# Moving the loads of the next batch's k and v behind the last store of a second layer

## The chip, the cores and the metric

The kernel runs on one core of one Trainium2 chip. The metric is the device time of one execution in microseconds (us). A single-core run gets the state "fast" unless it is over 1.5% above the fastest run of the same kernel.

## The reference

Linear attention without softmax, an RMS norm, then a gated feed-forward layer, all in fp32:

```python
# q, k, v: (8 batches, 8 heads, 576 tokens, 64)
kv  = einsum('bhsd,bhse->bhde', k, v)
out = einsum('bhsd,bhde->bhse', q, kv)
out = out / sqrt(mean(out*out, -1) + 1e-6) * g_norm
x   = out.transpose(0, 2, 1, 3).reshape(4608, 512)
gate = 1 / (1 + exp(-(x @ w_gate)));  val = x @ w_val          # 512 -> 1536
result = (gate * val) @ w_out                                  # 1536 -> 512
```

## The kernel before

The feed-forward layer goes over nine chunks of 512 tokens, c = 0 to 8. Each chunk has a first layer (`first_layer_fast`, pairs of blocks of 7 products each) and a second layer (`second_layer_fast`). The products of both are of a Strassen kind: 7 in place of 8. The attention of batch c+1 is fed into chunk c in small steps: a queue `fill`, from which `slot()` takes one step after each pair of products.

What the argument needs: k and v of batch c+2 are asked for at the end of chunk c, and used in chunk c+1.

```python
def load_late(b):                      # 12 transfers, all on SP's queue
    if b >= B: return
    for n in range(NHP):               # 8 of 128 x 512 fp32 (256 KB)
        for name, src in (("k", k), ("v", v)):
            mains[n, name] = t = hp.tile([P, G], FP32, tag="gv", name="kv")
            nc.sync.dma_start(out=..., in_=src[b, 2*n:2*n+2, 0:S4]...)          # L112
    rest = hp.tile([P, G], FP32, tag="gv", name="kv")
    for i, src in enumerate((k, v)):   # 4 of 64 KB
        for r in range(2):
            nc.sync.dma_start(out=rest[...], in_=src[b, ..., S4:S]...)          # L117
...
def feed(b):                           # steps of the attention of batch b, for fill
    ...
    steps = turns_of(n0) + turns_of(n0 + 1)        # 4 transposes on DVE
    if b > 2:
        steps += [(PE, idle)] * (7 - len(steps))
    steps += [(PE, kv_mm), (DVE, kv_out)]          # the k.v products: L347, L353
...
def sg_tile():
    return sb.tile([P, G], FP32, tag="sg", name="sg", bufs=4)
...
def first_layer_fast(c):               # in each block
    d["pa"] = pa = mm_ps()[:, h1]
    product(pa, bg[:, 0:NK], a[1, 1], True)                     # L693
    d["sg"] = sg_tile()
    nc.scalar.copy(out=d["sg"][:, h2], in_=pa)                  # L701: writes an sg buffer
    ...
def second_layer_fast(c):
    for g in range(2):
        ...                                                     # o2, o1 = sg_tile(), sg_tile()
        store(c, 2 + g, o2)
        if g == 1:
            load_late(c + 2)
        for pc, x in zip(pcs, parts):
            product(pc, lambda f: s4[c, f][:, t1], b[2, 2][:, :, x], False)
            tt(out=o1[:, y], in0=pc, in1=o1[:, y], op=ALU.add)  # L811
            ...
        if not last:
            store(c, g, o1)                                     # L488, L493
```

The pool `sg` has four buffers, A to D. The built program hands them out in a fixed round: the second layer's four tiles take C, B, A, D (o2 and o1 of g = 0, then o2 and o1 of g = 1), each read by a store. The next first layer's first pair of blocks takes C and B, its second pair A and D. So the L701 of the eighth step of that first layer writes D, the buffer that the last store reads.

Of the kernel before, what the change touches and what calls it, by code (L numbers as in the profile page):

```python
# [20 lines left out]
def kernel(  # L21
# [81 lines left out]
    def load_late(b):  # L103


        if b >= B:
            return
        mains = {}
        for n in range(NHP):
            for name, src in (("k", k), ("v", v)):  # L110
                mains[n, name] = t = hp.tile([P, G], FP32, tag="gv", name="kv")
                nc.sync.dma_start(out=t.rearrange("p (h c) -> p h c", h=2),  # L112
                                  in_=src[b, 2 * n:2 * n + 2, 0:S4].rearrange("h (p j) d -> p h (j d)", j=NK4))
        rest = hp.tile([P, G], FP32, tag="gv", name="kv")
        for i, src in enumerate((k, v)):
            for r in range(2):
                nc.sync.dma_start(out=rest[PH * r:PH * r + PH, GH * i:GH * i + GH].rearrange("p (h d) -> p h d", d=HD),  # L117
                                  in_=src[b, NHP * r:NHP * r + NHP, S4:S].rearrange("h p d -> p h d"))
        kv_late[b] = mains, rest
# [209 lines left out]
    def slot():  # L329
        if fill:  # L330
            fill.popleft()()
# [144 lines left out]
    def sg_tile():  # L476
        return sb.tile([P, G], FP32, tag="sg", name="sg", bufs=4)

    def store(c, t, ot, cols=slice(0, DM), queues=(nc.sync,)):

        r0 = i = 0
        while r0 < P:
            b, s = divmod(G * c + P * t + r0, S)
            rows = out[S * b:S * b + S, cols]
            if b < 2:
                j, p = divmod(s, NP)
                n = min(P - r0, NP - p)
                queues[i % len(queues)].dma_start(out=rows.rearrange("(p j) d -> j p d", j=NJ)[j, p:p + n],  # L488
                                                  in_=ot[r0:r0 + n, cols])
            else:  # L490
                r, c0 = divmod(s, QC)
                n = min(P - r0, QC - c0)
                queues[i % len(queues)].dma_start(  # L493
                    out=rows.rearrange("(r p j) d -> r j p d", p=QB, j=NJ)[r, c0 // QB:(c0 + n) // QB],
                    in_=ot[r0:r0 + n, cols])
            r0 += n
            i += 1
# [12 lines left out]
    def mm_ps():  # L510
        if next(turns) % 4 < 2:
            return psum.tile([P, 512], FP32, tag="mm", name="mm", bufs=2)
        return mm0_ps()
# [253 lines left out]
    def second_layer_fast(c):  # L767
        b = {(j, n): w2[:, NF2 * (j - 1):NF2 * j, DH * (n - 1):DH * n] for j in (1, 2) for n in (1, 2)}
        d1, d2 = slice(0, DH), slice(DH, DM)
        for g in range(2):  # L770
            t1, t2 = slice(P * g, P * g + P), slice(GH + P * g, GH + P * g + P)
            pa, pb = (mm_ps()[:, 0:DH] for _ in range(2))

            last = (c, g) == (NG - 1, 1)
            parts = [slice(0, DH // 2), slice(DH // 2, DH)] if last else [slice(0, DH)]

            def product(ps, hs, ws, new):
                for f in range(NF2):
                    nc.tensor.matmul(ps, hs(f), ws[:, f, :], start=(new and f == 0), stop=(f == NF2 - 1),  # L779
                                     skip_group_check=True)  # L780
                    if f % 3 == 2:
                        slot()

            product(pa, lambda f: gv[c, f][:, t1], b[1, 1], True)
            o2 = sg_tile()
            nc.scalar.copy(out=o2[:, d1], in_=pa)
            product(pb, lambda f: s12[c, f][:, t2], t2w[2], True)
            o1 = sg_tile()
            tt(out=o1[:, d2], in0=pb, in1=o2[:, d1], op=ALU.add)
            product(pa, lambda f: gv[c, f + NF2][:, t1], b[2, 1], False)  # L790
            nc.scalar.copy(out=o1[:, d1], in_=pa)
            if last:
                store(c, g, o1, d1)
            product(pb, lambda f: gv[c, f][:, t2], t2w[3], False)
            tt(out=o2[:, d2], in0=pb, in1=o2[:, d1], op=ALU.add)
            pcs = []
            for x in parts:
                pcs.append(mm_ps()[:, 0:x.stop - x.start])
                pc = pcs[-1]
                product(pc, lambda f: s12[c, f][:, t1], t2w[1][:, :, x], True)  # L800
                o2x = o2[:, DH + x.start:DH + x.stop]
                tt(out=o2x, in0=pc, in1=o2x, op=ALU.add)
            product(pb, lambda f: gv[c, f + NF2][:, t2], t2w[4], False)
            tt(out=o2[:, d1], in0=pb, in1=o2[:, d1], op=ALU.add)
            store(c, 2 + g, o2)
            if g == 1:
                load_late(c + 2)
            for pc, x in zip(pcs, parts):
                product(pc, lambda f: s4[c, f][:, t1], b[2, 2][:, :, x], False)
                y = slice(DH + x.start, DH + x.stop)  # L810
                tt(out=o1[:, y], in0=pc, in1=o1[:, y], op=ALU.add)  # L811
                if last:
                    store(c, g, o1, y, (nc.sync, nc.scalar))
            if not last:
                store(c, g, o1)

    def sums_of(c):
        if c < NG:
            fill.append(lambda: fill.extendleft(reversed(x_sums(c))))
# [31 lines left out]
    for c in range(1, NG):  # L851
        if c + 1 < B:
            steps = feed(c + 1)
            if c == 1:

                i = 5
                while w2_sums:
                    steps.insert(i, (DVE, w2_sums.popleft()))
                    i += 3
            spread(steps, (1, 2, 3, 4, 5) if c == 1 else (2, 3, 4, 5))  # L860
        first_layer_fast(c)
        sums_of(c + 1)
        second_layer_fast(c)
        flush()
# [30 lines left out]
```

## Time and profile before

| | |
|---|---|
| median of 4 runs | 1098.61 us (1098.3 to 1099.22) |
| span of the profiled run | 1100.3 us, granted clock 0.995 |
| TensorE (PE) busy | 98% |
| PE's waits for L701 | 6.0 us, 4 times |

In the profile PE is TensorE, ACT ScalarE, DVE VectorE, SP the engine whose queue issues the transfers. L693 is a line of the kernel. A wait row reads "engine, line that waited <- what released it: us in total, times, longest". A timeline row reads "start, duration, engine, line, operation, out<-in, count, [idle before <- releaser]"; "SPq" is SP's queue, and its duration is the issue alone. In the rows of windows the seventh value after the window's ends is the granted clock. The prediction shows the page, PE's waits, the chain and SP's queue; here is what it read without showing: ACT and PE at the end of chunk 2 in the timeline of the kernel before.

```profile
411.37 0.37 ACT L701 COPY sg<-mm 128x256 f32<-128x256 f32 x1 [1.71 <-PE mm L693]
...
414.75 0.37 ACT L701 COPY sg<-mm 128x256 f32<-128x256 f32 x1 [3.00 <-DMA out_dram<-sg]
...
415.17 1.13 PE L693 MATMUL mm<-xT,gv 128*128 128x256 f32 x4 [0.39 <-ACT sg L701]
416.23 2.08 PE L347 MATMUL at<-kv 128*64 128x64 f32 x64
```

The two L701 of a pair usually run 0.9 us apart. Here the second runs 3.4 us after the first, released by the store's landing. PE stops for it, because the third product of a block adds into the buffer `pa` that this L701 must have read. The k·v products (L347) start right after.

### The profile page before, as it was taken

The page shows a single profiled execution, that of the slowest core. Times are in us where ns is not written, and L with a number is a line of the kernel's source. Part 1 is how long each engine was busy: PE and PEld are TensorE (multiplying, and loading weights), DVE is VectorE, ACT ScalarE, POOL GpSimd, SP SyncE. Part 2 cuts the span into 40 slices and gives each one's busy share as a digit, 9 for nine tenths or more (in the row PEclk, how much of TensorE's full clock was granted, in tenths as well). Part 3 has the DMA queues.
Part 4 walks back from the last instruction along what each step waited for, and adds up shares of the span by engine and source line. Part 5 has one row for each costly group of instructions (what it writes and reads, how often), then busy time and mean ns, then how long its engine had stood idle before and what let it go on. Part 6 is the DMA issues. An engine that isn't in the chain of part 4 may idle for free.

```text
span 1100.3 us, 18225 instructions
## 1 busy us (share of the span) xinstructions
PE 1083.6 (98%) x7334; PEld 897.9 (82%) x7334; DVE 619.7 (56%) x1219; ACT 267.5 (24%) x545; POOL 289.9 (26%) x390
## 2 busy tenths in 40 slices
PE   8999999999999999999999999999999999999997
PEld 7644448888888888888788878888888888888886
DVE  3787756883486447652576248643765256515641
ACT  3654321132113311322123211331132111101210
POOL 0000024450254024420444024411442045304500
PEclk9999999999999999999999999999999999999999
DMA  9944711001400140002200040013000100010001
GB/s 245 266 153 153 238 29 32 1 8 35 128 1 8 34 120 10 1 23 86 61 1 23 21 127 1 1 32 116 22 1 1 30 10 1 1 33 8 0 2 38
DMA packets 57288, 57.80 MB, mean 53 GB/s; under 512 B 18548, under 2 KB 51188, under 8 KB 57204
## 3 DMA queue, kind: packets, MB, share of 16 engines
q1 hardware_dynamic: 57044, 56.64, 17.4%
q8 instruction: 58, 0.95, 0.3%
q14 instruction: 26, 0.21, 0.1%
q10 hardware_dynamic: 160, 0.00, 0.0%
HBM read 47.19 MB, written 9.44 MB: 51 GB/s over the span
## 4 chain that ended last, share of the span: by engine, by line
PE 93%; DMA 5%; SPq 1%; ACT 0%; issue 0%; DVE 0%; ACTq 0%
PE mm L693 49%; PE mm L779 26%; PE mm L540 7%; PE mm L637 4%; DMA out_dram<-sg 2%; PE at L391 2%; DMA kv<-in_v_dram 1%; PE at L347 1%; PE at L416 1%; DMA v<-in_v_dram 1%; DMA kv<-in_k_dram 1%; PE at L540 1%; PE two L255 0%; PE two L312 0%; PE two L285 0%; PE two L266 0%
## 5 line engine op out<-in xcount | busy, mean ns | idle before, releaser
L680 POOL TENSOR_TENSOR tw<-gv 128x256 f32<-128x256 f32 x192 | 139.3, 736 | 756.7 <-PE mm L693 601.2
L693 PE MATMUL mm<-xT,gv 128*128 128x256 f32 x768 | 182.5, 380 | 6.0 <-ACT sg L701 6.0
L693 PE MATMUL mm<-xT,tw 128*128 128x256 f32 x768 | 182.7, 380 | 0.2 <-issue 0.2
L693 PE MATMUL mm<-sx,tw 128*128 128x256 f32 x768 | 181.4, 379 | 0.0
L693 PEld LDWEIGHTS mm<-xT,gv 128*128 128x128 f32 x768 | 145.6, 190 | 27.6 <-ACT sg L701 7.6
L693 PEld LDWEIGHTS mm<-sx,tw 128*128 128x128 f32 x768 | 145.9, 190 | 19.8
L693 PEld LDWEIGHTS mm<-xT,tw 128*128 128x128 f32 x768 | 145.0, 190 | 20.6 <-issue 0.7
L680 POOL TENSOR_TENSOR tw<-gv,tw 128x256 f32<-128x256 f32 x192 | 155.8, 832 | 0.0
L725 ACT ACTIVATE sg<-sg 128x256 f32<-128x256 f32 x96 | 39.1, 417 | 239.6 <-DVE sg L724 239.3
L715 DVE TENSOR_TENSOR gv<-mm,sg 128x256 f32<-128x256 f32 x96 | 40.7, 424 | 89.6 <-PE mm L693 89.5
L693 PE MATMUL mm<-sx,gv 128*128 128x256 f32 x384 | 90.9, 380 | 0.0
L732 DVE TENSOR_TENSOR gv<-gv,sg 128x512 f32<-128x512 f32 x96 | 90.7, 983 | 0.0
L779 PE MATMUL mm<-w,s 128*128 128x256 f32 (+1 forms) x408 | 89.1, 367 | 0.0
L779 PE MATMUL mm<-w,gv 128*128 128x256 f32 x384 | 88.8, 380 | 0.0
L779 PE MATMUL mm<-t2w,gv 128*128 128x256 f32 x384 | 88.2, 379 | 0.0
L779 PEld LDWEIGHTS mm<-w,s 128*128 128x128 f32 x408 | 73.7, 190 | 9.1
L779 PEld LDWEIGHTS mm<-t2w,gv 128*128 128x128 f32 x384 | 72.8, 190 | 9.9
L779 PEld LDWEIGHTS mm<-w,gv 128*128 128x128 f32 x384 | 72.4, 190 | 10.0
L693 PEld LDWEIGHTS mm<-sx,gv 128*128 128x128 f32 x384 | 72.4, 190 | 9.7
L701 ACT COPY sg<-mm 128x256 f32<-128x256 f32 x96 | 35.8, 373 | 178.6 <-PE mm L693 165.1
L540 PE MATMUL mm<-xT,gv 128*128 128x512 f32 x176 | 77.4, 593 | 0.0
L711 ACT ACTIVATE sg<-mm 128x256 f32<-128x256 f32 x96 | 36.9, 384 | 111.0 <-PE mm L693 111.0
(99 smaller groups left out, 1038.2 us busy)
## 6 DMA issues: line engine op xcount, KB each, us to landing
q<-in_q_dram SPq DMA_DIRECT2D x24, 288.0 KB
st<-in_moe_w_gate_dram SPq DMA_DIRECT2D x12, 512.0 KB
st<-in_moe_w_val_dram SPq DMA_DIRECT2D x12, 512.0 KB
st<-in_moe_w_out_dram SPq DMA_DIRECT2D x12, 512.0 KB
kv<-in_k_dram SPq DMA_DIRECT2D x24, 256.0 KB
kv<-in_v_dram SPq DMA_DIRECT2D x24, 256.0 KB
out_dram<-sg SPq DMA_DIRECT2D x17, 256.0 KB
out_dram<-sg SPq DMA_DIRECT2D x25, 128.0 KB
```

The lines of the kernel that those rows point to most:

```text
L347: nc.tensor.matmul(ps[HD * e:HD * e + HD, n, 0:HD], mains[n, "k"][:, c], mains[n, "v"][:, c], start=(j == 0), stop=False)
L391: nc.tensor.matmul(u[PH * half:PH * half + PH, r, P * s + HD * e:P * s + HD * e + HD], qTs[QB * r:QB * r + QB, (n0 + which) % 2, c:c + PH] ...
L540: nc.tensor.matmul(self.ps[i], w[("wg", "wv")[i], self.f][:, m, :], xT[self.c][:, m, :], start=(m == 0), stop=(m == NMT - 1), skip_group_c ...
L637: nc.tensor.matmul(ps[t], gv[0, f][:, P * t:P * t + P], w["wo", f], start=(f == 0), stop=(f == NFT - 1), skip_group_check=True)
L680: nc.gpsimd.tensor_tensor(out=tw[f, i], in0=b[in0], in1=b[in1] if isinstance(in1, tuple) else tw[f, in1], op=ALU.subtract)
L693: nc.tensor.matmul(ps, wt[:, m, :], xs[:, m, :], start=(new and m == 0), stop=(m == NK - 1), skip_group_check=True)
L701: nc.scalar.copy(out=d["sg"][:, h2], in_=pa)
L711: nc.scalar.activation(out=d["sg"][:, h1], in_=d["pa"], func=AF.Sigmoid)
L715: tt(out=d["h"][:, h2], in0=d["pb"], in1=d["sg"][:, h2], op=ALU.add)
L725: nc.scalar.activation(out=d["sg"][:, h2], in_=d["sg"][:, h2], func=AF.Sigmoid)
L732: tt(out=d["h"], in0=d["h"], in1=d["sg"], op=ALU.mult)
L779: nc.tensor.matmul(ps, hs(f), ws[:, f, :], start=(new and f == 0), stop=(f == NF2 - 1), skip_group_check=True)
```

## The change

Intent: the last store of a chunk should not stand in SP's queue behind twelve loads that nobody needs for another 17 us.

```diff
             store(c, 2 + g, o2)
-            if g == 1:
-                load_late(c + 2)
             for pc, x in zip(pcs, parts):
                 ...
             if not last:
                 store(c, g, o1)
+            if g == 1:
+                load_late(c + 2)
```

L811 of the kernel before is L809 in the changed one; the other lines named here keep their numbers.

## The prediction

> **What bounds the kernel now.** I read the page first. TensorE (PE) is busy almost without a hole, and the chain that ended last runs through it, but with 5% of DMA in it:
>
> ```profile
> PE 1083.6 (98%) x7334; PEld 897.9 (82%) x7334; DVE 619.7 (56%) x1219; ACT 267.5 (24%) x545; POOL 289.9 (26%) x390
> ...
> PE 93%; DMA 5%; SPq 1%; ACT 0%; issue 0%; DVE 0%; ACTq 0%
> ```
>
> So only two things can move the time: the number of matmuls (the change leaves it; the listing of PE's instructions in order is the same in both kernels, 1087 rows of 1087) and the holes in PE. The next view is who PE waited for (total us, times, longest):
>
> ```profile
> PE mm L693 <- ACT sg L701: 6.0, 4, 2.7
> PE two L255 <- DMA v<-in_v_dram: 2.1, 1, 2.1
> PE mm L618 <- POOL ident masks.py:199: 1.4, 1, 1.4
> ```
>
> The last two belong to the start, before the changed line. The first is four holes inside the loop over chunks of 512 tokens: the first layer (L693) waits for the copy at L701. The chain in order of time says why. This is the end of chunk 4 (start us, us, what):
>
> ```profile
> 640.95 7.08 DMA kv<-in_v_dram
> ...
> 648.81 7.41 DMA out_dram<-sg
> ...
> 656.32 0.38 ACT sg L701
> 656.70 0.04 issue
> 656.75 1.13 PE mm L693 x4
> ```
>
> A load of v lands at 648.03; only then is the store of an output tile asked for; it lands 7.41 us later, at 656.22; only then may L701 write, because it takes over the buffer that the store read (the pool sg has four, and the second pair of first-layer blocks gets the pair that the last stores of the second layer read). Why does the store wait for a load? The timeline of the queue that asks for transfers (SP), end of chunk 2:
>
> ```profile
> 396.28 0.57 SPq L493 DMA_DIRECT2D out_dram<-sg  x1
> 396.89 0.47 SPq L112 DMA_DIRECT2D kv<-in_k_dram  x1
> ...
> 401.09 0.66 SPq L112 DMA_DIRECT2D kv<-in_k_dram  x1
> 403.82 0.37 SPq L112 DMA_DIRECT2D kv<-in_v_dram  x1
> 404.47 1.38 SPq L117 DMA_DIRECT2D kv<-in_k_dram  x2
> 405.90 1.27 SPq L117 DMA_DIRECT2D kv<-in_v_dram  x2
> 407.36 0.61 SPq L493 DMA_DIRECT2D out_dram<-sg  x1
> ```
>
> SP works in program order: first store, twelve loads, last store. The last store's data was ready when the DVE addition L811 ended (398.42 + 0.42 = 398.84), but it was asked for at 407.36: 8.5 us late. The order listing with waits shows eight completion semaphores taken in turn: a transfer waits until the one eight before it has landed. So the eighth load (403.82) waits for the first store, and the rest follow as earlier loads land, each some 7.2 to 7.6 us after its issue.
>
> **What the Trainium skill says.** "Perfetto Trace Analysis", DMA Instruction — HWDGE: the profiled window of such an instruction ends when its descriptors are made, and the data movement is outside it. The trace agrees: 0.61 us of issue, 7.4 us to landing. "DMA: Bandwidth & Descriptors", Anatomy of one DMA — SWDGE (gpsimd) path (the sentence is not limited to that path): DMA engines don't wait on semaphores; the issuing sequencer waits before dispatch. That is why one late lane holds up everything behind it, seen in the gap from 401.75 to 403.82. The same page, Rules for kernel authors: issue the DMA early and wait on it late. The kernel before does that for the loads at the store's cost. "TensorE: Matmul & The Clock Gate", Part 1: PE falls to half clock after an idle window of about 3.4 us that is free-running. The trace agrees on the half clock but shows it after a hole of only 2.4 us, at the end of chunk 3 (columns: window, PE busy, PEld, DVE, ACT, POOL, granted clock, DMA share, GB/s):
>
> ```profile
> 534.00:535.00 1.00, 0.00 (x0) 0.00 (x0) 0.00 (x0) 0.40 (x2) 0.00 (x0) 1.00 0.11 41
> ...
> 537.00:538.00 1.00, 1.00 (x24) 1.00 (x24) 0.00 (x0) 0.00 (x0) 0.00 (x0) 0.50 0.07 16
> ```
>
> **The change, part by part.** It moves twelve loads (eight of 256 KB, four of 64 KB) from ahead of the last store to behind it, at the end of chunks 1 to 5; chunks 6 to 8 load nothing. It adds and removes no instruction.
>
> *What it takes off.* I measure each hole by PE's own pace, not by the wait view: from the start of the first-layer block before the k·v products (L347) to their start. With no hole (end of chunk 1) that is 298.37 - 296.55 = 1.82 us. After chunks 2, 3, 4, 5 it is 2.47, 4.47, 4.81 and 2.58: too much by 0.65 + 2.65 + 2.99 + 0.76 = 7.05 us (the wait view has 6.0, for the restart costs a little too). At the end of chunk 3 the half clock adds: L347's 64 matmuls took 3.61 us there and 2.08 elsewhere, 1.53 more. Sum 8.6 us. All of it is on the path: PE is the chain there.
>
> Afterwards the last store goes out at about 398.9 and, with the same 7.4 us, lands at about 406.4; L701 wants its buffer at about 412.3 (0.9 us after the first of the pair, which ran at 411.37). Slack 6 us, so these four holes should go.
>
> *What it adds.* The loads start later: the store is ready at 398.84 and takes about 0.6 us to issue, so the first load goes at about 399.5 in place of 396.9, 2.6 us later. Estimate for chunk 2 with the lanes and 7.4 us: loads 1 to 6 at 399.5 to 402.3; load 7 waits for the first store (403.8); load 8 for the last store (406.4); the four small ones for loads 1 to 4 (407 to 409.3). Load 8 lands at 413.8, the small ones by 416.7 at most (they are a quarter of the size). PE without a hole reaches L347 at 413.76 + 1.82 = 415.6, the last pair of heads some 1.5 us later, and the small ones (L353) at 417.6. So they land 3 and 1 us ahead. The same sum for chunk 4, which has two first stores and slower issue, leaves 0 to 2 us; for chunk 3 about 1 to 3. I put the new waits at 0.5 us in all, from 0 to 3.
>
> The loads of q behind them also slip by about 2 us, but what they bring is used some 20 us later. The order on ACT, Pool and PE isn't touched.
>
> **Rivals.** (a) The wait moves: PE waits at L347 for k and v in place of L701. For it: my slack is 1 to 3 us and my landing times have errors of 1 us. Against it: before, nothing waited there, with loads issued by 407.2 and L347 at 416.2. If all five ends were 2 us late, that is +10 - 8.6: about 1100. (b) The holes of the timed runs are smaller than those of the profiled run, which took 1102.08 us against 1098.38: part of those 3.7 us may be slower transfers and so longer holes, and the half-clock event need not occur in each run. Then the gain is 4 to 6 us: 1092.5 to 1094.5. (c) All 8.6 us come back: 1089.8. (d) The store was hidden and L701 waits for something else. Against it, the trace names the store's landing for three of L701's waits (13.3 us in all, ACT's own idle), and each landing is within 0.1 us of L701.
>
> **Range and chances.** Middle of (b) and (c), less 0.5 for (a): 1098.4 - 8.6 + 0.5 = 1090.3 if the profiled holes are typical, about 1094 if not; I take 1091.5, weighting the first higher. Low 1089: everything comes back and a little more of PE's restart cost. High 1095.5: (b) together with some of (a). 2% would be 22 us. The holes in the changed stage sum to 8.6 us, so faster by 2% is out of reach; slower by 2% would take over 6 us of new wait at each of the five ends. Faster 0.01, same 0.98, slower 0.01.
>
> **What the changed profile would show.** Right: the row "PE mm L693 <- ACT sg L701" gone from PE's waits; SP's order store, store, loads, with the last store within 0.2 us of L811's end; the five distances to L347 all near 1.82 us; no 0.50 clock after chunk 3; the DMA share of the chain well under 5%. Wrong: a wait of L347 or L353 for the kv loads (rival a), or holes of a few us elsewhere in the first layer. The prediction fails on size if the holes vanish but the timed gain is under 4 us (rival b).

## The result, and the profile after

1090.08 us median of 4 runs (1089.43 to 1091.25) against 1098.61. The ratio is 0.9923, 95% interval 0.9906 to 0.994. A ratio here is the mean time of one kernel's fast runs over the mean time of the other's fast runs of the same rounds, so it is not quite the ratio of the medians quoted. The difference of the medians is 8.5 us.

The page of the changed kernel:

```profile
PE 1079.0 (99%) x7334; PEld 894.8 (82%) x7334; DVE 619.5 (57%) x1219; ACT 267.6 (25%) x545; POOL 289.9 (27%) x390
...
PE 99%; ACT 0%; DVE 0%; issue 0%; POOL 0%; POOLq 0%
```

No transfer is left in the rounded shares of the chain. PE's waits in the changed kernel, all of them:

```profile
PE mm L618 <- POOL ident masks.py:199: 1.4, 1, 1.4
PE two L285 <- ACT qTs L271: 0.6, 2, 0.3
```

The row of L701 is gone and nothing has come in its place: no row of L347 or L353. The timeline of the changed kernel at the end of chunk 2:

```profile
394.05 1.89 PE L693 MATMUL mm<-xT,gv 128*128 128x256 f32 x8
394.25 0.42 DVE L809 TENSOR_TENSOR sg<-mm,sg 128x256 f32<-128x256 f32 x1 [2.17 <-PE mm L779]
394.75 0.55 SPq L493 DMA_DIRECT2D out_dram<-sg  x1
...
395.41 0.45 SPq L112 DMA_DIRECT2D kv<-in_k_dram  x1
...
402.94 0.37 SPq L112 DMA_DIRECT2D kv<-in_v_dram  x1
...
405.04 1.27 SPq L117 DMA_DIRECT2D kv<-in_v_dram  x2
...
408.11 0.37 ACT L701 COPY sg<-mm 128x256 f32<-128x256 f32 x1 [0.54 <-PE mm L693]
...
411.41 2.08 PE L347 MATMUL at<-kv 128*64 128x64 f32 x64
```

The store goes out 0.08 us after L809's end (394.25 + 0.42 = 394.67), where before it went out 8.5 us after. The L701 that used to be late follows the first of its pair by 0.9 us and is released by PE. The other signs that the prediction named are there too: all five distances to L347 are 1.82 us, and no half clock is left between the chunks. The first load goes out 1.36 us after the first-layer block starts (395.41 - 394.05); before it was 1.33 us ahead of it (396.89 - 398.22). That is 2.7 us later, and the last small loads are issued some 3 us later; nobody waits for them.

Where the time went can be summed. From one start of L347 to the next, in the chains of both kernels:

| from the k·v products of chunk ... to the next | before | changed | less |
|---|---|---|---|
| 2 (end of chunk 1) to 3 | 298.44 to 416.30: 117.86 | 294.27 to 411.48: 117.21 | 0.65 |
| 3 to 4 | 416.30 to 536.16: 119.86 | to 528.83: 117.35 | 2.51 |
| 4 to 5 | 536.16 to 657.88: 121.72 | to 646.04: 117.21 | 4.51 |
| 5 to 6 | 657.88 to 775.84: 117.96 | to 763.25: 117.21 | 0.75 |

Together 8.4 us, against 8.5 us between the timed medians. The two profiled spans differ by more, 12.7 us. The other 4.2 us lie before the first k·v products of the loop, at 174.19 us in one trace and 170.00 in the other, where both programs are the same. In ten other traces that start lies between 169.8 and 173.3; the run of the changed kernel with 173.3 was also the slowest of its runs (1093.12). So the start varies from run to run and is no part of the change.

### The profile page after: what moved, and what is told of

Same layout as the page of the kernel before. It is cut to its first block, busy times and chain, and to the rows that moved or that the text cites. A ratio compares the mean times of both kernels' runs of the same rounds, so it can differ in the third digit from the quotient of the medians.

```text
span 1087.6 us, 18236 instructions
## 1 busy us (share of the span) xinstructions
PE 1079.0 (99%) x7334; PEld 894.8 (82%) x7334; DVE 619.5 (57%) x1219; ACT 267.6 (25%) x545; POOL 289.9 (27%) x390
## 4 chain that ended last, share of the span: by engine, by line
PE 99%; ACT 0%; DVE 0%; issue 0%; POOL 0%; POOLq 0%
PE mm L693 54%; PE mm L779 27%; PE mm L540 7%; PE mm L637 4%; PE at L391 2%; PE at L347 1%; PE at L416 1%; PE mm L618 1%; PE at L540 1%; PE two L285 1%; PE two L255 1%; PE two L312 0%; PE two L266 0%; PE at L353 0%; ACT qTs L271 0%; DVE ms L294 0%
## 5 line engine op out<-in xcount | busy, mean ns | idle before, releaser
L725 ACT ACTIVATE sg<-sg 128x256 f32<-128x256 f32 x96 | 39.1, 417 | 238.0 <-DVE sg L724 237.7
L701 ACT COPY sg<-mm 128x256 f32<-128x256 f32 x96 | 35.7, 372 | 164.4 <-PE mm L693 164.2
```

The costliest lines, as they stand in the source:

```text
L725: nc.scalar.activation(out=d["sg"][:, h2], in_=d["sg"][:, h2], func=AF.Sigmoid)
```

## The experiments

Times come with runs of the kernel before on the same chip, with medians of before of 1098.41 (1096.01 to 1102.04, 11 runs), 1099.78 (1098.31 to 1103.93, 11 runs) and 1098.15 (1095.73 to 1100.25, 7 runs). All results were correct.

**1. The changed kernel again** (label r_after; no edit).

> The changed kernel again, for a tighter interval and a second profile. Theory (the holes at L701 are the whole gain): 1098.6 - 8.6 = 1090.0 us, ratio 0.992, the five distances from the first-layer block to the k-v products (L347) all 1.82 us. Rival (part of the 12.7 us by which the two profiled spans differ is the change too): under 1088. I expect the extra 4.2 us of the spans to sit ahead of the first products, where the kernels are the same, and to differ from run to run.

1090.4 us median of 6 (1089.72 to 1093.12), ratio 0.9927 (0.9909 to 0.9945). The five distances to L347 were 1.81 to 1.82 us. PE waited for L701 nowhere, and the extra length of one span lay at the start, as said above. The result stands.

**2. Six sg buffers, loads left where they were** (label e1_six_sg; edit against the kernel before).

```diff
-        return sb.tile([P, G], FP32, tag="sg", name="sg", bufs=4)
+        return sb.tile([P, G], FP32, tag="sg", name="sg", bufs=6)
```

> The kernel before with six sg buffers in place of four, loads still ahead of the last store. Theory (the late store hurts only because L701 takes over its buffer): all holes go, 1090 us, though the last store is still asked for some 8.5 us late. Rival (PE loses time from the order of the transfers itself, by memory traffic or the queue): 1098.6, holes stay.

1089.91 us (1089.37 to 1093.6, 6 runs), ratio 0.993 (0.9911 to 0.9948), no hole. In its trace the last store of chunk 2 still goes out behind the loads (first load at 392.80 us, store at 403.26), and L701 runs at 408.18, 4.9 us after that issue, without PE stopping. That is before the store has landed: its last completion record in the packed trace is at 410.59. (These records, one set for each transfer, are in the trace file, but no view of `prof` prints them; "landing" below means the last of them, where no view is shown.) So the order of transfers itself cost nothing. The late store cost time only through the buffer that it held.

**3. Only the four small loads behind the store** (label e2_small_behind; edit against the kernel before, shortened).

```diff
             store(c, 2 + g, o2)
             if g == 1:
-                load_late(c + 2)
+                load_late(c + 2, True)          # the 8 of 256 KB
 ...
             if not last:
                 store(c, g, o1)
+            if g == 1:
+                load_rest(c + 2)                # the 4 of 64 KB
```

> Only the four small loads of each chunk go behind the last store; the eight of 256 KB stay ahead. The store should go out some 2.9 us earlier than before, at about +5.7 us from the end of L811 in place of 8.5. Theory (a hole is the store's landing less the time when L701 wants the buffer): the holes of 0.65, 2.65, 2.99, 0.76 us shrink to 0, 0, 0.1, 0, so 1090 to 1091. Rival (the holes depend on the large loads being in flight with the store): most of them stay, 1095 to 1098.

1090.43 us (1090.02 to 1090.69, 5 runs), ratio 0.9928 (0.9911 to 0.9945). PE has no hole at L701. The timelines of the SP queue and of ACT, end of chunk 2 (L500 is the store and L708 the copy in this file):

```profile
400.89 0.55 SPq L500 DMA_DIRECT2D out_dram<-sg  x1
...
409.09 0.37 ACT L708 COPY sg<-mm 128x256 f32<-128x256 f32 x1 [0.99 <-DMA out_dram<-sg]
```

The copy does wait for the store's landing, 0.5 us longer than usual, and PE does not stop: there is a little room between a late copy and a hole. Taking four of the twelve loads, 256 KB of 2.3 MB, from ahead of the store is enough.

**4. The change at the ends of chunks 3 and 4 alone** (label e4_only_3_4).

```diff
-            if g == 1:
+            if g == 1 and c not in (3, 4):
                 load_late(c + 2)
 ...
             if not last:
                 store(c, g, o1)
+            if g == 1 and c in (3, 4):
+                load_late(c + 2)
```

> The change at the ends of chunks 3 and 4 alone; chunks 1, 2 and 5 as before. Theory (the sum of holes, each chunk for itself): 2.65 + 2.99 + 1.53 (half clock) = 7.2 us come back, 1091.4, and holes of about 0.7 us stay after chunks 2 and 5. Rival (the holes of one chunk carry over to the next): other holes change size too.

1091.66 us (1091.42 to 1092.2, 5 runs), ratio 0.994 (0.9923 to 0.9958): 6.75 us back by the medians, of the 7.2 expected. PE's waits:

```profile
PE mm L693 <- ACT sg L701: 1.1, 2, 0.6
```

Two holes are left, after chunks 2 and 5, of 0.75 and 0.9 us by the distances of L347 against 117.21. Each chunk end pays for itself.

**5. The k·v products three steps earlier in the changed kernel** (label e3_kv_early3).

```diff
         if b > 2:
-            steps += [(PE, idle)] * (7 - len(steps))
-        steps += [(PE, kv_mm), (DVE, kv_out)]
+            steps += [(PE, kv_mm)] + [(PE, idle)] * 3 + [(DVE, kv_out)]
+        else:
+            steps += [(PE, kv_mm), (DVE, kv_out)]
```

> The changed kernel, with the k-v products (L347, L353) of batches 3 to 7 three first-layer steps (5.2 us) earlier, all else in place. It measures the slack that my prediction put at 1 to 3 us: if so, PE waits 2 to 4 us for k and v at each of five chunk ends and the time is 1100 to 1110 us. Rival (the loads land more than 5 us ahead): no wait, 1090.

1100.69 us (1100.38 to 1103.52, 4 runs), ratio 1.0014 (0.999 to 1.0039): 10.4 us slower than run 7, which equals the changed kernel. Now PE waits for v, and the time is in the expected 1100 to 1110. The end of chunk 3 in PE's timeline, one line for each pair of heads:

```profile
525.78 0.69 PE L347 MATMUL at<-kv 128*64 128x64 f32 x16 [0.48 <-DMA kv<-in_v_dram]
527.17 0.69 PE L347 MATMUL at<-kv 128*64 128x64 f32 x16 [0.70 <-DMA kv<-in_v_dram]
528.42 0.69 PE L347 MATMUL at<-kv 128*64 128x64 f32 x16 [0.57 <-DMA kv<-in_v_dram]
530.12 0.69 PE L347 MATMUL at<-kv 128*64 128x64 f32 x16 [1.01 <-DMA kv<-in_v_dram]
```

By the start of the first-layer block after them, the products were finished late by 0, 1.2, 3.7, 3.0 and 0.9 us after chunks 1 to 5, 8.7 us in all, and the block after those of chunk 4 took 3.63 us in place of 1.99, at half clock: 10.4 us. The products were moved forward by 5.2 us. Taking these delays off, the loads land over 5.2, then 4.0, 1.5, 2.2 and 4.3 us ahead of the old need. After chunk 4 it was not only L347 that waited: L353, which needs the small loads, waited 0.3 us more. The rival of the prediction, waits that move to L347 or L353, was that close after chunks 3 and 4.

**6. The k·v products nine steps earlier** (label e7_kv_first; a single run with a profile, state unknown).

```diff
         if b > 2:
-            steps += [(PE, idle)] * (7 - len(steps))
-        steps += [(PE, kv_mm), (DVE, kv_out)]
+            steps = [(PE, kv_mm)] + steps + [(PE, idle)] * 4 + [(DVE, kv_out)]
+        else:
+            steps += [(PE, kv_mm), (DVE, kv_out)]
```

> The changed kernel, with the k-v products of batches 3 to 7 nine steps (15.6 us) earlier, so that PE surely waits: the start of L353 then shows when the loads have landed. Expected from 7.4 us a landing: the eighth large load 14 to 15 us after the end of L809, the small ones 14 to 18 us after; a wait of 12 to 15 us at each of five ends, 1150 to 1165 us, half clock after each. If the loads land within 11 us of L809, the slack was over 5 us.

1160.88 us. PE's timeline after chunk 2 shows the landings of the four pairs directly:

```profile
406.39 1.89 PE L694 MATMUL mm<-xT,gv 128*128 128x256 f32 x8
417.06 1.12 PE L347 MATMUL at<-kv 128*64 128x64 f32 x16 [8.79 <-DMA kv<-in_v_dram]
...
421.29 1.12 PE L347 MATMUL at<-kv 128*64 128x64 f32 x16 [0.37 <-DMA kv<-in_v_dram]
422.34 0.71 PE L353 MATMUL at<-kv 64*64 64x64 f32 x16
```

The eighth large load lets PE go 14.9 us after the start of the first-layer block (421.29 - 406.39), 16.2 after chunk 3 and 14.7 after chunk 5. In the changed kernel L347 starts 17.3 us after that start, and its last pair 1.5 us later, so that load is due at 18.8. So it is 3.9, 2.6 and 4.1 us ahead, which agrees with run 5 within about 1 us. Here L353 does not wait: the small loads had landed before the last large one was worked off. The expectation was met: the eighth load comes 14.3 us after L809's end, and the time is 70.6 us above run 7, 14 us for each chunk end, half clock included.

**7. The last store asked for by ACT, loads not held behind it** (label e5_store_act; edit against the changed kernel).

```diff
             if not last:
-                store(c, g, o1)
+                store(c, g, o1, queues=(nc.scalar,) if g == 1 and c + 2 < B else (nc.sync,))
             if g == 1:
                 load_late(c + 2)
```

> The changed kernel with the last store of chunks 1 to 5 asked for by ACT in place of SP, so that the loads do not wait in SP's order for L809 to end: both the early loads and the early store. Theory (PE has no hole left to fill): the same 1090 us, loads starting about 2.6 us earlier. Rival (the loads' later start costs something elsewhere): 1 us or more faster. ACT pays about 0.6 us of issue per store, which should lie in its idle time.

1090.28 us (1089.36 to 1090.58, 6 runs), ratio 0.991 (0.9894 to 0.9926). In its trace of chunk 2 the first load goes out at 393.04 us and the store, on ACT, at 395.05, taking 1.16 us of issue. Both are early, and it is no faster than the change: with no hole left, earlier loads buy nothing.

**8. The last store later still, as first tried** (label e6_store_later; edit against the kernel before).

```diff
             if not last:
-                store(c, g, o1)
+                if g == 1 and c + 2 < B:
+                    held.append(lambda c=c, g=g, o1=o1: store(c, g, o1))
+                else:
+                    store(c, g, o1)
 ...                                        # in the first layer of the next chunk
                 slot()
+                if held and i == 6:
+                    held.pop()()
```

> The kernel before with the last store of chunks 1 to 5 still later, behind two loads of q as well: asked for some 2.5 us later than before. Theory (each hole grows by what the store slips): holes of about 0.6 to 1.5, 3.1, 5.1, 5.5, 3.3 us after chunks 1 to 5, together 18 us against 7; with half clock after those over 2.4 us another 1.5 us each: 1098.6 + 11 + 3 to 5 = 1112 to 1115. Rival (the store is not what L701 waits for): no change, 1098.6.

This missed: 1090.08 us (1089.21 to 1090.9, 4 runs), ratio 0.9909 (0.989 to 0.9929), no hole. Taken at its word it spoke for the rival that L701 does not wait for the store. Its SP queue and ACT timelines (L703 is the copy in this file), end of chunk 2:

```profile
406.35 0.62 SPq L493 DMA_DIRECT2D out_dram<-sg  x1
...
408.43 0.37 ACT L703 COPY sg<-mm 128x256 f32<-128x256 f32 x1 [0.49 <-PE mm L695]
```

The store was indeed late, and the copy ran 2.1 us after its issue, 3.7 us before it landed (412.12). The built program shows why. With the store placed inside the next first layer, the buffer of o1 comes free later in program order, and the pool no longer gives it to the second pair of blocks: after chunk 1 that pair gets A and C, where C was the first pair's, and D goes out only to the third pair; after later chunks it is the same with other letters. So the edit changed two things, and the second undid the dependence that the first was to stretch. The edit is a third way to the same gain, and no test of the theory. That needed a store that is later with the buffers in the old order.

**9. Four more loads ahead of the store, buffers in the old order** (label e8_four_more; edit against the kernel before, shortened: the pool `sums` is also opened earlier). Four loads of 64 KB into a spare tile that nobody reads; the built program gives out C, B, A, D as before.

```diff
+    spare = sums.tile([P, 4, 2 * HD], FP32, name="spare", bufs=1)
 ...
             if g == 1:
                 load_late(c + 2)
+                if c + 2 < B:
+                    for h in range(4):
+                        nc.sync.dma_start(out=spare[:, h],
+                            in_=k[c + 2, h, 0:2 * P].rearrange("(p j) d -> p (j d)", j=2))
```

> The kernel before, with four more loads of 64 KB (into a spare tile that nobody reads) between the twelve loads and the last store of chunks 1 to 5, and, other than in the run that moved the store, the same sg buffers in the same order. At one load per 0.65 us the store goes out some 2.6 us later than before. Theory (a hole is the store's landing less the time when L701 wants its buffer): the holes grow by about 2.6 us each, to 3.2, 5.2, 5.6, 3.4 us after chunks 2 to 5 and 0 to 2 after chunk 1, 17 to 20 us against 7; with half clock after three to five of them, 1.5 us each: 1112 to 1117. Rival (the store is not what PE waits for, as the run that moved it seemed to say): 1098 to 1099.

1112.17 us (1111.43 to 1113.7, 4 runs), ratio 1.0126 (1.0108 to 1.0145). PE's waits, then the end of chunk 2 in the timeline:

```profile
PE mm L693 <- ACT sg L701: 15.8, 4, 5.3
```

```profile
406.61 0.62 SPq L493 DMA_DIRECT2D out_dram<-sg  x1
...
413.97 0.37 ACT L701 COPY sg<-mm 128x256 f32<-128x256 f32 x1 [5.48 <-DMA out_dram<-sg]
...
414.40 1.41 PE L693 MATMUL mm<-xT,gv 128*128 128x256 f32 x4 [2.86 <-ACT sg L701]
```

Counted from the start of the next first layer in the timelines (394.97 here, 398.22 in the kernel before), the store went out 11.6 us after it in place of 9.1: 2.5 us later. The four holes grew from 0.39, 2.38, 2.72, 0.49 to 2.86, 4.80, 5.29, 2.84 us, each by 2.4 to 2.6, 9.8 together. Half clock took part of the rest: L347 and the four matmuls before it cost 5.4 us more than at full clock, in place of 1.5. 9.8 + 3.9 = 13.7 us, and the clock says 14.0. After chunk 1 there was still no hole.

**10. The same four loads and six sg buffers** (label e9_four_more_six_sg; run 9's edit with run 2's).

> The same four more loads ahead of the store, with six sg buffers. Theory (only the buffer that the store still reads holds L701): no hole, 1090 us, though the store goes out latest of all. Rival (the traffic of more loads slows PE, or the k-v products wait): 1092 or more.

1089.59 us (1089.55 to 1089.98, 4 runs), ratio 0.992 (0.9906 to 0.9935), no hole, with the store going out as late as in run 9 (at 405.88 us in its trace of chunk 2). Runs 9 and 10 differ in the buffers alone and in 22.6 us. What stopped PE was the buffer that the late store still read, and nothing else about the store or the loads.

No run beats the change: six buffers, the split loads, the store on ACT and the moved store all end within 0.8 us of it, inside the spread, for in all of them PE has no hole left in the loop.

## Why the prediction was right

The time, 1090.08 us, lay in the range; the predicted 1091.5 was 1.4 too high.

- **The bound and the mechanism** held. Runs 2, 9 and 10 show that the hole at L701 is the store's landing against the reuse of its buffer; run 9 that it follows the store's issue one to one.
- **The 8.6 us** were right: 8.4 in the traces, 8.5 by the clock. Run 4 gave 6.75 of the 7.2 for two of the five ends. Measuring by PE's pace and not by the wait rows (6.0) made the difference: the wait rows count neither the restart nor the half clock.
- **The later loads** were right at 2.6 us (measured 2.7), and the slack of 1 to 3 us was about right where it was least: 1.5 after chunk 3 and 2.2 after chunk 4 by run 5. The landings in the changed kernel's own trace give 1.7 and 1.0 us there, with the small loads as the tightest each time; after chunks 1, 2 and 5 they give 6.9, 3.0 and 4.1. So after chunk 2 the slack was larger than the predicted 1 us, because the loads asked for last land sooner than the full 7.4 us that I used as a bound (after chunk 2 the eighth took 6.6, the small ones 4.8 to 6.1).
- **Two readings were loose**, though nothing rests on them. Not every transfer lands 7.2 to 7.6 us after its issue: in the kernel before, after chunk 2, the first seven large loads took 7.1 to 7.8 us, but the eighth 5.6 and the small ones 3.9 to 5.1, and after chunk 3 the second half of the last store took 8.55. And the cut in the chain of chunk 4 leaves out two pieces, an addition on DVE (L724) and an activation on ACT (L725), which the store does not need, so these lines don't show that it waited for a load. The completion records do: the transfer eight before it, the load issued at 639.90, landed at 648.74, and the store went out at 648.81.
- **The term that was mis-sized** is rival (a), "the new waits at 0.5 us in all": none in the profile.
- **Rival (b)**, that timed holes are smaller than profiled ones, was given too much weight: it alone pulled the middle from 1090.3 to 1091.5. The difference of the medians equals the sum of the profiled holes, though to 0.1 us that is luck, given the spread of the kernel before. Part of (b) stays possible: 6 of the 29 runs of the kernel before took 1095.7 to 1096.7 us, some 2 us less than most. Runs without the half clock, which cost 1.5 us, would look like that; none of them was profiled. The profiled run's extra length that suggested (b) fits the start, which differed by 4.2 us between two traces.
- **Rival (d)**, that L701 waits for something else, seemed to be supported by run 8 and fell with runs 9 and 10.

One question that the holes raise, when a hole of 2.4 to 2.9 us lowers the clock and when it does not, the traces answer for L701. In each trace looked at (the kernel before, runs 5, 6 and 9), the changes of the clock lie whole steps of 3.413 us apart. In the kernel before, half clock lasts from 20.67 to 24.08 us and from 536.08 to 539.50, and 536.08 is 150 steps after 24.08. Laid on these steps, the holes after chunks 3 and 4 look like this (rows of windows; the second value after the window's ends is PE's busy time):

```profile
532.67:536.08 3.41, 1.05 (x4) 0.68 (x4) 0.47 (x2) 0.66 (x2) 0.00 (x0) 1.00 0.10 36
536.08:539.50 3.42, 3.42 (x65) 3.42 (x64) 0.00 (x0) 0.38 (x1) 0.00 (x0) 0.50 0.02 5
...
652.13:655.55 3.42, 1.89 (x9) 1.33 (x7) 1.90 (x6) 0.00 (x0) 0.00 (x0) 1.00 0.44 142
655.55:658.96 3.41, 2.21 (x42) 1.83 (x44) 0.42 (x1) 1.04 (x3) 0.00 (x0) 1.00 0.09 31
```

The hole of 2.38 us falls into one step, which leaves PE 1.05 us of work in it, and the next step runs at half clock. The longer hole of 2.72 us is split over two steps (1.89 and 2.21 us of work), and the clock stays. Run 9 agrees: its holes of 2.86, 4.80 and 5.29 us leave steps with 0.72, 0.00 and 0.00 us of work, each followed by half clock, the last for two steps; its hole of 2.84 us is split (1.97 and 2.01), and the clock stays. So in these two traces what counted was where the hole lay in the steps. It stays open why a step of run 5 with 2.18 us of work, much of it in small matmuls, was followed by half clock too, when another there with 1.77 was not.

## What to carry to other kernels

SP's queue issued its transfers in program order here, so what stood ahead of a store also delayed the buffer that the store gave back; look at who takes that buffer next before putting loads first. Order transfers by the slack of their consumers: here the store had about none behind the loads, and the loads had 1 to 7 us to spare behind the store. When an edit moves the last use of a tile in program order, look at which buffer the pool then gives to whom, since the edit may remove the very dependence that it should test.

## What the Trainium skill lacked or had wrong

- "TensorE: Matmul & The Clock Gate", Part 1, puts half clock after at least one idle window of about 3.4 us, and lets the windows run freely. The traces show the free-running steps of 3.41 us, but not that a window must be idle: windows with 1.05 us (kernel before, chunk 3) and 0.72 us (run 9, chunk 2) of PE work, around holes of 2.38 and 2.86 us, were followed by a granted clock of 0.50. The two holes that were split over two windows (2.72 and 2.84 us, with 1.89 us of work or more in each window) were not. Half clock lasted one window, or two (run 9, chunk 4), and cost 1.5 to 2.4 us.
- "DMA: Bandwidth & Descriptors", Anatomy of one DMA, has a landing time for one transfer on the path issued from GpSimd. No page read here has one for a burst issued from SP: in the kernel before, after chunk 2, the first seven loads of 256 KB each landed 7.1 to 7.8 us after their issue, which is an estimate of 283 GB/s for eight in flight (8 x 262,144 bytes in 7.4 us). The last store of 256 KB behind the loads took as long, 7.3 to 7.4 us after chunks 2, 4 and 5. After chunk 1 the loads took only 3.0 to 5.7 us.
- No page read here speaks of the transfer that waits for the one eight before it, because completion semaphores are taken in turn: the eighth load after chunk 2 went out at 403.82, when the first store had landed (403.75). That left SP's queue empty for 2.1 us (401.75 to 403.82), and for 3.0 us after chunk 4.
- No page read here speaks of the order in which a pool hands out buffers; it decided run 8 (1090.08 us, where 1112 to 1115 was expected).
